# A hand-ordered S5 scan and GEGLU kernel: a filler product taken out, two transposes moved ahead of the parameters, and two loads moved back behind slab 0's first gated rows

## The chip, the cores and the metric

The kernel runs on one core of one Trainium2 chip. The metric is the device time of one execution in microseconds (us). Below, PE is the matrix engine (TensorE; PEld are its weight loads), DVE the vector engine, ACT the scalar engine, POOL GpSimd, and SP the engine that issues nearly all transfers, in the order in which the program lists them.

## What is computed

```python
x  = A_x                                  # 1 x 2048 x 512, bf16
xn = (x - mean(x)) / sqrt(var(x) + 1e-5)  # over the 512 columns
# S5 scan over the 2048 rows, state of 512 complex numbers
Lam_bar = exp(exp(log_dt) * (Lambda_re + 1j * Lambda_im))
Bu = xn @ (((Lam_bar - 1) / Lam)[:, None] * B).T
h[t] = Lam_bar * h[t - 1] + Bu[t]
s  = 2 * real(h @ C.T) + xn * Dskip
# gated feed-forward, 512 -> 1376 -> 512
g  = silu((gelu(xn @ w_gate) * (xn @ w_up)) @ w_down)
out = x + s * g
```

## The kernel before

The 2048 rows are cut into four slabs of 512 rows, and each slab into four tiles of 128 rows. Per slab the kernel normalizes the rows, turns them (columns onto partitions), multiplies them by w_up and w_gate (`gate_tile`; for slab 0 `up_rows` and `first_w`), multiplies the two results into `at`, turns `at` into `atT` by a transposing transfer (`at_t`), multiplies by w_down (`down_pair`), projects with B (`half`, which also holds the scan on DVE), and joins everything in `y_tile`.

**The order is written out by hand.** Every piece of work is a step with a number, given in the order in which `Plan.add` is called; `ORDER` lists the numbers in the order in which they are put into the program. An engine executes its own steps strictly in that order, so only the order within one engine matters; a step waits there for whatever it reads and for the buffers that it writes.

The start, where the change is. Slab 0 is not normalized before its first products: `center` subtracts the mean (tile 0 with sums on DVE and ACT, tiles 1 and 2 with a sum on ACT and the subtraction on DVE, L351), `head_t` turns the tile on PE with four small products against the identity matrix, and DVE or ACT copies the result out of PSUM into `xcT` (L322 and L324 for the two halves of tile 0, L333 for tiles 1 and 2). `up_rows(m, k)` is a pair of products of tile m with the k-th 128 rows of w_up, and can run as soon as that quarter of w_up has landed. The inverse deviation is applied when the products are copied out.

- Step 26, `dummies`: seven products of constants, before any data is there.
- Steps 30, 31: tile 0 turned on PE (L316). Step 34, `parameters` (L606, L607): log_dt and Lambda turned, into `ybank[1]`. Step 60, `fill` (L305): one product of constants into `ring[0]`, which nothing reads. Step 61: tile 1 turned (L331), into `ybank[0]`. Step 63: `up_rows(0, 0)`. Step 65: tile 2 turned, into `ybank[1]`. Step 64: `up_rows(1, 0)`; the other pairs follow.
- On DVE: step 41 (tile 1 centered, L351), 35 (the parameters copied out of `ybank[1]`, L609), 32 (first half of tile 0 copied, L322), 43 (tile 2 centered), 62 (tile 1 copied), 66 (tile 2 copied).

The loads on SP: x tiles 0 to 2, four quarters of w_up, its last columns, x tile 3, and w_gate in two parts (steps 0 to 10). Then step 115 (L686): the last 96 of w_down's 1376 rows, 96 KB; step 113 (L217): x of slab 1, 512 KB; step 116 (L687): `Drow`, the 512 values of Dskip copied to all partitions, 128 KB. Then transposing transfers: step 137 (L367), slab 0's normalized rows into `xnT`; steps 11 and 12 (L237), B's real and imaginary part into `BT`; step 152 (L468), the gated rows of tile 0 into `atT`. Step 114 (L685): w_down's first 1280 rows, 1280 KB. Steps 153 and 154: tiles 1 and 2 into `atT`. Step 224: slab 1 into `xnT`.

What uses them: PE needs `xnT` of slab 0 for `first_w(3, ...)` (L421) and for `half(0, ...)` (L550, which also needs `BT`); `down_pair(0, ...)` (L484) takes tile 0, then tile 2, then tile 1, eleven products each, the first ten with w_down's first 1280 rows and the last with the 96. `Drow` is read by `skip` on DVE (L372), steps 130, 132, 134, 136 for the four tiles of slab 0.

Of the kernel before, what the change touches and what calls it, by code (L numbers as in the profile page):

```python
# [18 lines left out]


ORDER = (
    21, 22, 23, 24, 25, 0, 27, 26, 20, 18, 19, 17, 1, 40, 15, 16, 13, 14, 2, 42, 3, 4, 5, 28, 29, 30, 31, 34, 60, 33, 44, 45, 41, 61, 35, 32, 63, 43,
    65, 62, 64, 69, 68, 66, 67, 71, 72, 46, 47, 36, 37, 38, 48, 49, 50, 52, 51, 55, 54, 129, 56, 6, 74, 77, 70, 73, 80, 75, 76, 78, 79, 53, 81, 82, 7,
    83, 85, 87, 84, 118, 86, 120, 88, 8, 57, 58, 131, 133, 59, 135, 119, 39, 194, 195, 117, 121, 122, 9, 89, 91, 93, 90, 92, 94, 10, 95, 97, 101, 103,
    107, 109, 96, 98, 102, 104, 108, 110, 115, 113, 212, 213, 216, 217, 123, 99, 100, 210, 211, 214, 215, 218, 116, 136, 132, 105, 106, 219, 130, 111,
    112, 134, 125, 124, 126, 137, 138, 140, 142, 144, 146, 148, 139, 141, 143, 145, 147, 149, 150, 151, 11, 156, 160, 175, 157, 161, 220, 225, 12,
    158, 162, 177, 179, 159, 181, 223, 163, 222, 221, 176, 178, 354, 182, 180, 164, 165, 166, 168, 167, 169, 170, 171, 172, 173, 174, 183, 152, 114,
    229, 230, 153, 154, 233, 231, 234, 224, 237, 239, 254, 271, 279, 276, 275, 272, 278, 240, 255, 232, 273, 274, 277, 280, 281, 155, 235, 241, 292,
    260, 243, 236, 242, 288, 256, 238, 196, 197, 198, 261, 298, 258, 293, 307, 289, 257, 294, 244, 299, 313, 303, 200, 184, 199, 201, 259, 296, 290,
    308, 304, 318, 295, 297, 311, 322, 309, 291, 305, 185, 187, 282, 186, 188, 226, 202, 203, 204, 314, 348, 312, 326, 328, 228, 227, 301, 300, 323,  # L30
    337, 205, 206, 207, 306, 320, 310, 324, 327, 319, 333, 286, 321, 335, 341, 283, 325, 284, 285, 329, 128, 316, 189, 208, 191, 192, 209, 193, 349,
    343, 355, 315, 190, 331, 330, 350, 360, 361, 339, 334, 127, 342, 336, 338, 356, 245, 246, 351, 362, 250, 302, 414, 422, 287, 372, 376, 374, 389,
    373, 377, 340, 378, 393, 390, 344, 391, 406, 416, 375, 379, 394, 417, 421, 415, 392, 420, 407, 345, 346, 357, 249, 248, 365, 247, 252, 253, 353,
    262, 263, 332, 410, 431, 411, 366, 432, 371, 251, 317, 352, 358, 347, 412, 439, 446, 408, 440, 419, 413, 441, 395, 418, 409, 437, 435, 447, 442,
    456, 454, 396, 436, 450, 433, 457, 438, 452, 477, 451, 471, 423, 265, 424, 425, 428, 434, 448, 467, 426, 461, 455, 475, 367, 449, 429, 453, 267,
    266, 264, 444, 476, 478, 498, 469, 269, 270, 462, 496, 268, 363, 359, 427, 443, 472, 459, 499, 468, 488, 492, 458, 368, 482, 489, 497, 493, 470,
    369, 480, 380, 381, 384, 382, 383, 463, 364, 430, 533, 473, 519, 490, 515, 474, 494, 483, 491, 520, 495, 521, 522, 516, 503, 479, 385, 464, 386,
    484, 370, 485, 500, 387, 501, 388, 397, 398, 399, 401, 402, 445, 547, 535, 517, 504, 548, 518, 509, 510, 531, 534, 532, 511, 505, 400, 404, 403,
    405, 523, 524, 527, 526, 514, 528, 465, 481, 460, 549, 486, 502, 553, 551, 537, 554, 565, 559, 552, 536, 555, 538, 550, 561, 557, 563, 560, 574,
    615, 558, 556, 570, 566, 620, 621, 572, 616, 580, 571, 564, 562, 576, 573, 587, 581, 595, 578, 585, 579, 593, 575, 589, 577, 591, 568, 594, 596,  # L40
    610, 506, 525, 512, 529, 567, 487, 583, 617, 625, 626, 608, 507, 618, 582, 622, 630, 611, 590, 592, 606, 604, 588, 586, 600, 602, 631, 609, 603,
    605, 601, 607, 530, 539, 540, 613, 597, 541, 569, 513, 623, 508, 598, 627, 466, 644, 612, 543, 544, 542, 545, 546, 632, 619, 584, 638, 636, 639,
    599, 640, 624, 633, 628, 614, 642, 645, 643, 650, 651, 637, 646, 656, 657, 641, 661, 662, 666, 667, 634, 635, 629, 647, 652, 653, 658, 659, 663,
    664, 668, 669, 648, 649, 654, 655, 660, 665, 670,
)


# [33 lines left out]
def kernel(  # L81
# [103 lines left out]
    def pe(n, cols, emit, reads=(), writes=(), **kw):  # L185
        return pl.add(PE, n * (cols + 6) / 2400.0, emit, reads, writes, lag=0.22, **kw)
# [98 lines left out]
    def rstd(m0, m1):  # L285

        def f():
            if m0 in BN:
                G.tensor_scalar(out=ve[:, m0:m1], in0=mv[:, m0, 1:2], scalar1=EPS, scalar2=None, op0=ALU.add)
            else:  # L290
                G.tensor_scalar(out=ve[:, m0:m1], in0=ss[:, m0:m1], scalar1=1.0 / D, scalar2=EPS, op0=ALU.mult, op1=ALU.add)
            G.tensor_tensor(out=rs[:, 0, m0:m1], in0=ve[:, m0:m1], in1=mhalf[:, m0:m1], op=ALU.pow)
        return pool(0.65 + 0.2 * (m1 - m0), f, [("mv", m) if m in BN else ("ss", m) for m in range(m0, m1)] + ["mhalf"], [("rs", 0, m) for m in range(m0, m1)],
             rank=250.0 - 20 * m0)
# [7 lines left out]
    def fill(k, i):  # L302
        def f():
            for _ in range(k):
                T.matmul(ring[i][:], lhsT=warm[:, 0:P], rhs=warm, start=True, stop=True)  # L305
        pe(k, 512, f, [], [("bank", i)])

    def head_t(m):

        if m == 0:  # L310
            for i in range(2):
                tp = ring[2 + i][:].bitcast(BF16)[:, 0 : D // 2].rearrange("p (k t) -> p k t", t=P)

                def f(i=i, tp=tp):
                    for k in range(2):
                        T.transpose(tp[:, k, :], xn[0][:, (2 * i + k) * P : (2 * i + k + 1) * P], ident[:])  # L316
                pe(2, P, f, [("xc", 0, i), "ident"], [("bank", 2 + i)])
            for i in range(2):
                tp = ring[2 + i][:].bitcast(BF16)[:, 0 : D // 2].rearrange("p (k t) -> p k t", t=P)
                dst = xcT[:, 2 * i : 2 * i + 2, 0:P]  # L320
                if i == 0:
                    head.append(dve(256, lambda tp=tp, dst=dst: V.tensor_copy(out=dst, in_=tp), [("bank", 2)], [("xcT", 0, 0)], rate=2.0, rank=500.0, after=head[-1:]))  # L322
                else:
                    acts(256, lambda tp=tp, dst=dst: act(out=dst, in_=tp, func=AF.Copy), [("bank", 3)], [("xcT", 0, 1)], rank=500.0)  # L324
            return
        bank, key = ybank[(m + 1) % 2], ("y", (m + 1) % 2)
        tp = bank[:].bitcast(BF16)[:, 0:D].rearrange("p (k t) -> p k t", t=P)

        def f():
            for k in range(KT):  # L330
                T.transpose(tp[:, k, :], xn[m][:, k * P : (k + 1) * P], ident[:])  # L331
        pe(KT, P, f, [("xc", m, 0), ("xc", m, 1), "ident"], [key])
        dve(512, lambda: V.tensor_copy(out=xcT[:, :, m * P : (m + 1) * P], in_=tp), [key], [("xcT", m, 0), ("xcT", m, 1)], rate=2.0, rank=310.0 - 20 * m)  # L333
# [331 lines left out]
        rstd(m, m + 1)  # L665
    stats(M - 1)
    rstd(M - 1, M)
    fill(1, 0)
    head_t(1)
    up_rows(0, 0)  # L670
    up_rows(1, 0)
# [174 lines left out]
```

## Time and profile before

| | us |
|---|---|
| median of 3 runs | 178.81 |
| the runs | 178.15 to 179.05 |
| the profiled execution, whole | 178.7 |
| its span, first to last instruction | 176.9 |

Between the span and the whole execution lie 1.8 us in which no engine of the program works. The granted clock of PE over the span has the mean 0.998. The page counts how long each engine was busy, the chain of waits follows the work back from the last instruction, and the timeline lists instructions by their start. Most packets are small ones of 256 B, those of the transposing transfers:

```profile
DMA packets 48467, 18.66 MB, mean 105 GB/s; under 512 B 40296, under 2 KB 47944, under 8 KB 48456
```

When a transfer has landed is told by the trace's completion marks, sixteen for each transfer of full width; "landed" below means the last of them.

### The profile page before, as it was taken

The numbers are of one execution on the slowest core, as the hardware profiler recorded it, in microseconds if no ns is written. First come the engines' busy times: TensorE is split into PE (matmuls) and PEld (weight loads), VectorE is DVE, ScalarE is ACT, GpSimd is POOL, SyncE is SP. The second block draws the span as 40 slices with busy tenths as digits, with TensorE's granted clock in tenths as the row PEclk, the third lists the DMA queues.
The fourth block names the chain that finished last, engine by engine and source line by source line (L and its number), as shares of the span: only waits on it lengthen the run. The fifth ranks groups of instructions, "written<-read, shape, count | busy, mean of one in ns | idle before, by whom it ended". The sixth has DMA issues, their size and how long they took to land.

```text
span 176.9 us, 2403 instructions
## 1 busy us (share of the span) xinstructions
PE 172.0 (97%) x830; PEld 82.6 (47%) x846; DVE 157.0 (89%) x252; ACT 123.8 (70%) x236; POOL 11.3 (6%) x25
## 2 busy tenths in 40 slices
PE   8999999999999999999999999999999999999992
PEld 2554554444455544444445454444444455444451
DVE  3759999999798993999979999899999999999764
ACT  6499969969999999799578855373158618582240
POOL 2660030000200000000040000000000000000000
PEclk9999999999999999999999999999999999999999
DMA  5999999997000809423000074094000007718022
GB/s 150 311 372 230 201 235 261 205 284 143 0 0 0 200 1 186 98 79 62 0 0 6 30 139 93 31 191 85 0 0 0 0 30 158 68 34 160 26 76 76
DMA packets 48467, 18.66 MB, mean 105 GB/s; under 512 B 40296, under 2 KB 47944, under 8 KB 48456
## 3 DMA queue, kind: packets, MB, share of 16 engines
q1 hardware_dynamic: 48432, 18.52, 48.7%
q8 instruction: 6, 0.10, 0.3%
q14 instruction: 5, 0.04, 0.1%
q10 hardware_dynamic: 24, 0.00, 0.0%
HBM read 6.46 MB, written 2.10 MB: 48 GB/s over the span
## 4 chain that ended last, share of the span: by engine, by line
PE 94%; DVE 2%; DMA 1%; issue 1%; DVEq 0%
PE ring L452 31%; PE ring L484 21%; PE ring L550 16%; PE ybank L500 15%; PE ring L421 5%; PE ring L391 3%; PE ybank L421 2%; DMA x_tok<-in_A_x_dram 1%; DVE yg L505 1%; DVE junk L511 1%; PE ybank L331 0%; PE ring L316 0%; DVE yg L344 0%; PE ring L305 0%; DVE xna L346 0%
## 5 line engine op out<-in xcount | busy, mean ns | idle before, releaser
L452 PEld LDWEIGHTS <-xnT 128*128 128x128 bf16 x288 | 28.2, 98 | 28.4
L484 PE MATMUL ring<-wd,atT 128*128 128x512 bf16 (+1 forms) x171 | 38.9, 379 | 0.3
L452 PE MATMUL ring<-wg,xnT 128*128 128x512 bf16 (+1 forms) x142 | 31.4, 356 | 0.1
L452 PE MATMUL ring<-wu,xnT 128*128 128x512 bf16 (+1 forms) x142 | 31.2, 356 | 0.1
L550 PE MATMUL ring<-xnT,BT 128*128 128x512 bf16 x128 | 30.1, 379 | 0.0
L581 DVE TENSOR_TENSOR_SCAN Fs<-rho,ini,W 128x512 bf16<-128x512 f32 x24 | 29.7, 1271 | 0.1
L455 ACT ACTIVATE ub<-ring 128x512 bf16<-128x512 f32 (+1 forms) x36 | 19.2, 555 | 14.1 <-PE ring L452 14.0
L500 PE MATMUL ybank<-C,hst 128*128 128x512 bf16 x115 | 27.3, 379 | 0.3
L484 PEld LDWEIGHTS <-atT 128*128 128x128 bf16 (+1 forms) x176 | 17.2, 98 | 20.8
L552 ACT ACTIVATE U<-ring 128x512 bf16<-128x512 f32 x32 | 18.2, 600 | 7.5 <-PE ring L550 7.5
L455 ACT ACTIVATE gt<-ring 128x512 bf16<-128x512 f32 (+1 forms) x36 | 19.5, 555 | 3.7 <-PE ring L452 3.5
L500 PEld LDWEIGHTS <-hst 128*128 128x128 bf16 x136 | 13.3, 98 | 14.0
L550 PEld LDWEIGHTS <-BT 128*128 128x128 bf16 x128 | 12.5, 98 | 14.7
L487 ACT ACTIVATE g<-ring 128x512 f32<-128x512 f32 x16 | 9.4, 595 | 14.2 <-PE ring L484 14.2
L562 DVE TENSOR_TENSOR Q<-U,tab 128x4096 bf16<-128x4096 bf16 x8 | 18.3, 2289 | 0.9 <-ACT tab L649 0.7
L562 DVE TENSOR_TENSOR Q<-Fs,tab 128x4096 bf16<-128x4096 bf16 x8 | 18.3, 2287 | 0.1
L505 DVE TENSOR_TENSOR yg<-ybank,g 128x512 bf16<-128x512 f32 x15 | 10.2, 686 | 5.8 <-PE ybank L500 5.7
L764 ACT ACTIVATE junk<-x_tok 128x512 bf16<-128x512 bf16 x16 | 10.0, 633 | 0.8 <-DMA x_tok<-in_A_x_dram 0.8
L496 ACT ACTIVATE ybank<-sk 128x512 f32<-128x512 bf16 x15 | 9.1, 604 | 1.7 <-DVE yg L505 1.6
L769 ACT ACTIVATE xna<-x_tok,nb,rs 128x512 bf16<-128x512 bf16 x12 | 9.5, 812 | 0.0
L581 DVE TENSOR_TENSOR_SCAN Fs<-rho,W 128x512 bf16<-128x512 f32 x8 | 9.3, 1210 | 0.1
L461 DVE TENSOR_TENSOR at<-gt,ub 128x1024 bf16<-128x1024 bf16 x12 | 8.2, 684 | 0.1
(140 smaller groups left out, 170.6 us busy)
## 6 DMA issues: line engine op xcount, KB each, us to landing
x_tok<-in_A_x_dram SPq DMA_DIRECT2D x3, 512.0 KB, 4.1
out_dram<-ot SPq DMA_DIRECT2D x11, 128.0 KB, 1.8
wd<-in_B_w_down_dram SPq DMA_DIRECT2D x1, 1280.0 KB
wu<-in_B_w_up_dram SPq DMA_DIRECT2D x4, 256.0 KB, 4.1
wg<-in_B_w_gate_dram SPq DMA_DIRECT2D x1, 864.0 KB
x_tok<-in_A_x_dram SPq DMA_DIRECT2D x4, 128.0 KB, 2.1
wg<-in_B_w_gate_dram SPq DMA_DIRECT2D x1, 512.0 KB, 6.3
out_dram<-ot SPq DMA_DIRECT2D x6, 64.0 KB, 1.6
```

What stands on the lines that cost most here:

```text
L421: T.matmul(ps[:, 0 : b - a], lhsT=lhs(k), rhs=wt[:, k, a:b], start=(k == 0), stop=(k == KT - 1))
L452: T.matmul(ps[:, 0 : b - a], lhsT=xnT[:, s % 2, m, k, :], rhs=wt[:, k, a:b], start=(k == 0), stop=(k == KT - 1))
L455: acts(b - a, lambda: act(out=dst[:, a:b], in_=ps[:, 0 : b - a], func=AF.Copy if up else AF.Gelu_apprx_tanh), [("bank", r)], [key], table= ...
L484: T.matmul(ps[:], lhsT=atT[:fs, k, m * P : (m + 1) * P], rhs=wd[:fs, k, :], start=(k == 0), stop=(k == NFT - 1))
L500: T.matmul(ps, lhsT=hst[s % 2][:, j // NPT, j % NPT, m * P : (m + 1) * P], rhs=C2[:, j // NPT, j % NPT, c0:c1], start=(j == 0 and not seed ...
L505: dve(w, lambda: V.tensor_tensor(out=yg[e][:, c0:c1], in0=ps, in1=g2[gi][:, b, c0:c1], op=ALU.mult), [key, ("g2", gi, b)], [("yg", e, c0)])
L550: T.matmul(ps[:], lhsT=BT[:, ri, k, pt * P : (pt + 1) * P], rhs=xnT[:, s % 2, :, k, :], start=(k == 0), stop=(k == KT - 1))
L552: acts(512, lambda q=q, ri=ri, ps=ps: act(out=U[ui][:, ri, q, :], in_=ps[:], func=AF.Copy), [("bank", r)], [("U", ui, q, ri)])
L562: dve(4096, lambda: V.tensor_tensor(out=Qf, in0=src.unsqueeze(1).to_broadcast(WQ), in1=table, op=ALU.mult), reads, ["Q"], rate=2.0)
L581: pl.add(DVE, 1.12 if s == 0 else 1.185, lambda ri=ri, q=q, pt=pt, first=first: V.tensor_tensor_scan(out=Fs[:, ri, q, :], data0=rho[:, pt ...
L764: acts(512, lambda i=i, fn=fn, sc=sc, m=m: act(out=junk()[:], in_=x_tok[:, s * M + m, :], func=fn, scale=sc, accum_out=sx[:, s, i, m : m + ...
L769: acts(512, lambda m=m: act(out=xn[m], in_=x_tok[:, s * M + m, :], func=AF.Identity, scale=rs[:, s, m : m + 1], bias=nb[:, s, m : m + 1]), ...
```

## The change

One step goes, and some change place; nothing else in the code differs. Steps after 60 are numbered one lower afterwards; the text keeps the numbers of before.

```diff
     stats(M - 1)
     rstd(M - 1, M)
-    fill(1, 0)
+
     head_t(1)
     up_rows(0, 0)
```

```diff
 ORDER = (
-    21, 22, 23, 24, 25, 0, 27, 26, 20, 18, 19, 17, 1, 40, 15, 16, 13, 14, 2, 42, 3, 4, 5, 28, 29, 30, 31, 34, 60, 33, 44, 45, 41, 61, 35, 32, 63, 43,
-    65, 62, 64, 69, 68, 66, 67, 71, 72, 46, 47, 36, 37, 38, 48, 49, 50, 52, 51, 55, 54, 129, 56, 6, 74, 77, 70, 73, 80, 75, 76, 78, 79, 53, 81, 82, 7,
...
+    21, 22, 23, 24, 25, 0, 27, 26, 20, 18, 19, 17, 1, 40, 15, 16, 13, 14, 2, 42, 3, 4, 5, 28, 29, 30, 31, 33, 44, 45, 41, 60, 34, 32, 62, 43, 61, 35,
+    64, 63, 68, 67, 65, 66, 70, 71, 46, 47, 36, 37, 38, 48, 49, 50, 52, 51, 55, 54, 128, 56, 6, 73, 76, 69, 72, 79, 74, 75, 77, 78, 53, 80, 81, 7, 82,
...
```

Sorted by engine, in the numbers of before (ACT and POOL keep their order):

| engine | before | after |
|---|---|---|
| PE | 30, 31, 34, 60, 61, 63, 65, 64 | 30, 31, 61, 34, 63, 65, 64 |
| DVE, start | 41, 35, 32, 43, 62, 66 | 41, 32, 43, 62, 35, 66 |
| SP | 10, 115, 113, 116, 137, 11, 12, 152, 114, 153, 154, 224 | 10, 113, 137, 11, 12, 152, 116, 114, 115, 153, 154, 224 |
| DVE, later | 214, 215, 136, 132, 105, 106, 219, 130, 111, 112, 134, 125, 124, 126, 150 | 214, 215, 105, 106, 125, 219, 111, 112, 130, 136, 134, 132, 124, 126, 150 |

Steps 214 and 215 are the statistics of slab 1, 105 and 106 the gated rows of tile 1 (L434, L436), 111 and 112 those of tile 2, 150 those of tile 3, 219 slab 1's means (L760), and 124 to 126 three passes over the rotation tables (L642).

## The prediction

> **What bounds the kernel now.** I read the page's busy times, then the chain of waits, then the start and the stretch from 12 to 34 us in the timelines of PE, DVE and SP.
>
> ```profile
> PE 172.0 (97%) x830; PEld 82.6 (47%) x846; DVE 157.0 (89%) x252; ACT 123.8 (70%) x236; POOL 11.3 (6%) x25
> PE 94%; DVE 2%; DMA 1%; issue 1%; DVEq 0%
> ```
>
> PE is the bound, and the chain has hardly a gap: from 4.03 us until the tail at 172 us PE runs on. Whatever moves PE's sequence early on moves the end by as much, unless PE then waits for something that was just in time. So two questions: how much earlier can PE be at the start, and what does it then run into?
>
> The start, as the chain and the timelines of PE and DVE show it:
>
> ```profile
> 4.03 0.61 PE ring L316 x4
> 4.71 0.61 PE L305 MATMUL ring<-const-bfloat16-1.0 128*128 128x512 bf16 x1
> 5.12 0.62 PE L331 MATMUL ybank<-ident,xna 128*128 128x128 bf16 x4
> 5.54 0.62 PE L391 MATMUL ring<-wu,W 128*128 128x512 bf16 x2
> 6.25 4.92 PE L391 MATMUL ring<-wu,W 128*128 128x512 bf16 x22
> 4.04 0.35 DVE L351 TENSOR_SCALAR xna<-x_tok,ma 128x512 bf16<-128x512 bf16 x1
> 4.82 0.17 DVE L609 CAST pf<-ybank 128x12 f32<-128x12 bf16 x1 [0.43 <-PE ybank L607]
> 4.90 0.28 DVE L322 COPY W<-ring 128x256 bf16<-128x256 bf16 x1
> 5.10 0.34 DVE L351 TENSOR_SCALAR xna<-x_tok,ma 128x512 bf16<-128x512 bf16 x1
> 5.77 0.42 DVE L333 COPY W<-ybank 128x512 bf16<-128x512 bf16 x1 [0.33 <-PE ybank L331]
> ```
>
> The reader is to see two speeds of PE. The filler (L305) holds PE from 4.71 to 5.12, 0.41 us for 512 columns; the 22 products from 6.25 come every (4.92 - 0.38) / 21 = 0.216 us, with 0.38 the last one's own length. The trace's record of the granted clock begins at 5.58 us: before it PE runs at half speed. Tile 1 is centered by 4.39 us (4.04 + 0.35), yet its transposes wait behind parameters and filler.
>
> The second stretch, on SP and PE:
>
> ```profile
> 6.52 0.91 SPq L686 DMA_DIRECT2D wd<-in_B_w_down_dram  x1
> 7.48 0.73 SPq L217 DMA_DIRECT2D x_tok<-in_A_x_dram  x1
> 8.25 1.10 SPq L687 DMA_DIRECT2D Drow<-in_A_Dskip_dram  x1
> 12.45 3.42 SPq L367 DMA_TRANSPOSE xnT<-xna  x1
> 20.88 1.74 SPq L468 DMA_TRANSPOSE atT<-at  x1
> 22.66 0.63 SPq L685 DMA_DIRECT2D wd<-in_B_w_down_dram  x1
> 23.85 7.11 SPq L468 DMA_TRANSPOSE atT<-at  x2
> 31.32 7.30 PE L484 MATMUL ring<-wd,atT 128*128 128x512 bf16 x32
> 24.00:28.50 4.50, 4.50 (x23) 2.13 (x22) 4.47 (x8) 3.27 (x7) 0.00 (x0) 1.00 0.94 268
> ```
>
> By the completion marks the transfers land in the order of issue: Drow 16.06, `xnT` 19.57, B 21.30 and 23.21, `atT` of tile 0 24.74, w_down's 1280 rows 30.18, `atT` of tile 1 32.17, of tile 2 33.18. PE's first use of `xnT` is a weight load at 19.62. L484 takes tile 2 second, eleven products after 31.32: its first product starts at 33.70, and its weights are loaded from 33.48. So `atT` of tile 2 is 0.30 us ahead of its use, `xnT` 0.05 us. Both are just in time.
>
> **The change, part by part.**
>
> *Filler out, tile 1 first (PE).* Tile 1's four transposes can start at 4.45 (centered at 4.39, and 0.055 us from DVE to PE, as between L346's end at 3.97 and the weight load at 4.02), 0.107 us each at the slow clock. The parameters' pair follows; before it came 0.25 us after the fourth transpose's start and the next product 0.14 us later, so PE is free at 5.16. The first quarter of w_up landed at 5.13 (issued 2.11, 3.0 us), so `up_rows(0, 0)` starts at about 5.18 instead of 5.54: 0.36 us. But those 0.36 us are at half speed. By 5.58 before, 0.04 us of that pair was done; after, 0.40. At the full clock that is 0.18 us, so tile 2's transposes start at 5.81 instead of 6.00. They write the bank that the parameters' copy on DVE must have left: L322 at 4.67 at the latest (after all of L316), L351 of tile 2 at 4.89 (its sum is read on ACT by 4.86), L333 at 5.16, L609 at 5.51 to 5.68: 0.1 us before it is needed. Then `up_rows(1, 0)`: before, PE waited for L333 (ended 6.195) until 6.25; now 6.04. So far 0.21 us.
>
> *What it runs into.* The fourth quarter of w_up was issued at 3.54 and landed at 8.75. Its first product is the thirteenth of the run and started at 8.85. It cannot come before about 8.77. The transfers in front of it are untouched. So **0.08 to 0.10 us** is left of the gain: take -0.10. The parameters are read later by POOL (L610 from 5.07 to about 5.75, 1.03 us long); L611 needed it only at 7.58, so 0.8 us of cover remain, and without that cover the tables come late, not PE.
>
> *96 KB and 128 KB out of the first queue.* `xnT` was issued at 12.45, when DVE had the last normalized row, and then waited behind them. At 268 GB/s (the window's last number) 229 kB are 0.86 us. `xnT`, and behind it B, land 0.9 us earlier, 1.2 at best. PE does not wait for them today, so this gives nothing but margin: cost 0, hidden behind L421 and L550. The next gated tile, step 152, waits for DVE's L436, which ended at 20.72, and SP was free at 20.78: so it is issued at 20.8 as before, now into an empty queue. Its latency was 3.86 us; the like one at 56.30 took 3.5. It lands 0.1 to 0.45 earlier.
>
> *The same 224 KB put in front of tiles 1 and 2's transposes.* Three SP instructions then stand before step 153: Drow's issue (1.10), w_down's (0.63) and the last rows' (0.91), where only w_down's stood: step 153 is ready on DVE at about 23.2, is issued at 24.3 to 25.4, and steps 154 and 224 queue behind it. The data take 0.86 us by the window, or 0.95 by w_down's own pace (1280 KB from 24.74 to 30.18, 235 KB per us). Against that 0.1 to 0.45 gained above. Drow's issue also delays w_down's by up to 1.1 us, hidden while Drow's own 0.5 us and the transposes of tile 0 occupy the queue; at worst 0.6 us of it shows. `atT` of tile 2 therefore lands between 33.18 + 0.86 - 0.45 = 33.6 and 33.18 + 0.95 + 0.6 - 0.1 = 34.6; below that only if the queue's slack at 24 us (DMA share 0.94 in the window) takes some 0.3 us, 33.3. I take 33.9, near the data term, because 22.66 to 24.74 was already covered. PE wants it at 33.48 - 0.10 = 33.38, so it stands still for 0.5 us, with 0.05 us of weight load laid bare: **+0.55**. w_down's 1280 rows land near 30.8, wanted at 31.2; the last rows are wanted only at the eleventh product, 33.3.
>
> *Skips and tables moved on DVE.* Same instructions, same sum. Skip 130 now waits for Drow (about 25.5) at 25.2; behind it are the other skips, the tables and tile 3's gated rows (29.04 before, next used by a transfer at 34.33). DVE then idles 1.17 us at 46.70 waiting for ACT, which takes up such a delay. Cost 0; without that cover, up to 0.5 us late at the scan. Slab 1's `xnT` lands near 36.3, wanted at 38.46: covered.
>
> **Sum.** 178.7 of the profiled execution (span 176.9, 1.8 around it) - 0.10 + 0.55 = 179.15, say 179.2. The profiled execution lies 0.1 below the median of the runs, within their spread of 0.9, so I leave it there.
>
> **Rivals.** (1) *No stall:* tile 2 lands by 33.4, as tile 0's transfer goes into an empty queue and Drow fills slack. For it: the 0.45; against it: 0.86 us of data for 0.3 of margin. 178.6. (2) *Slower, a serial SP:* Drow's issue is not covered, tile 2 lands at 34.6 or later and PE stands still for 1.2 us at L484: 178.7 - 0.1 + 1.25 = 179.85, up to 180.4 if the last rows' issue shows as well. For it: 1.10 is SP's slowest copy; against: that was into a full queue. It is slower than before beyond doubt once the landing passes 34.3. (3) *The clock comes later.* Between 3.7 and 5.16 us PE now has transposes only. The filler was the one full product there. If the grant moves by d, PE loses d / 2; d is at most the 4.8 us from the first product (0.76) to the grant, so up to 2.4, 1.2 in the middle: 179.8 to 181. Against it: PE is no idler than before. (4) *Faster:* `xnT` has 0.05 us of margin in this execution; in others PE may wait for it, and the change ends that. At most the runs' spread, 0.9: 177.8.
>
> On the third: the Trainium skill, "TensorE: Matmul & The Clock Gate", Part 4, says that transposes do not count as PE activity for the clock in the same way, and Part 1 puts the window at some 3.4 us; by these one more window at half speed would cost an estimated 1.7 us, 180.3. The trace has the grant 4.8 us after the first product, with the filler in between, and cannot tell.
>
> **How the numbers follow.** What a measurement of this kernel can tell is about 0.5%, 0.9 us, hence "same" is 177.9 to 179.7. Chances: the forecast 0.34 (178.8 to 179.6), no stall 0.14, serial SP 0.30, later clock 0.10, faster 0.12. Same 0.34 + 0.14 = 0.48; slower 0.30 + 0.10 = 0.40; faster 0.12. The range 178.0 to 180.4 leaves out most of the faster case and the far half of the later clock.
>
> **What would show it.** L305 gone, L331 at 4.45 and L391 at 5.18; the product of w_up's fourth quarter at 8.77; `xnT` landing before 18.8; a wait of PE in L484 near 33.4 for `atT`, about 0.5 us, and tile 2's transposes landing at 33.9. If the first L391 run starts late, or the clock's record later than 5.6, rival 3 is right; if L484 has no gap, rival 1; a forecast of a gap elsewhere I do not make, and one at L421 or L550 would prove me wrong.

## The result, and the profile after

| | before | after |
|---|---|---|
| median, us (11 runs each, side by side) | 178.73 | 179.93 |
| the runs | 178.15 to 179.18 | 179.12 to 180.39 |
| ratio after to before, 95% interval | | 1.0059 (1.0038 to 1.0080) |
| the profiled execution, whole | 178.70 | 179.34 |
| its span | 176.9 | 177.5 |

The changed kernel is slower by 0.6%, 1.2 us, and the interval is clear of 1. The profiled execution of the changed kernel took 179.34 us, 0.6 below the median, so the trace below shows 0.64 us of the loss.

The page's busy times and the shares of its chain of waits:

```profile
PE 173.4 (98%) x845; PEld 82.5 (46%) x845; DVE 156.9 (88%) x252; ACT 123.5 (70%) x236; POOL 12.7 (7%) x25
PE 78%; DVE 8%; DMA 8%; SPq 2%; POOL 1%; issue 1%; DVEq 0%
```

PE is still busy nearly throughout, but its share of the chain fell from 94% to 78%, and transfers went from 1% to 8%. The chain itself (start, length, what) says which:

```profile
22.19 4.98 DMA Drow<-in_A_Dskip_dram
27.19 1.43 DVE sk L372 x4
28.62 1.05 DVE Q L642
29.68 4.46 DMA atT<-at
34.19 4.93 PE ring L484 x22
```

PE runs on from 34.19, released by a transposing transfer into `atT`. The two DVE lines in the middle are to be read with care: the chain follows the last releaser that it can infer, and says that DVE held up the issue of that transfer. SP was issuing the transfer before it until then, as the timelines of SP and DVE show:

```profile
20.36 1.79 SPq L468 DMA_TRANSPOSE atT<-at  x1
22.19 0.58 SPq L687 DMA_DIRECT2D Drow<-in_A_Dskip_dram  x1
22.82 0.44 SPq L685 DMA_DIRECT2D wd<-in_B_w_down_dram  x1
23.30 0.66 SPq L686 DMA_DIRECT2D wd<-in_B_w_down_dram  x1
24.06 7.90 SPq L468 DMA_TRANSPOSE atT<-at  x2
```

```profile
27.19 1.43 DVE L372 TENSOR_TENSOR sk<-xna,Drow 128x512 bf16<-128x512 bf16 x4 [1.36 <-DMA Drow<-in_A_Dskip_dram]
```

Issuing is short: 0.58 us for `Drow`, 0.44 and 0.66 us for w_down's two parts. What is long is `Drow` itself, which has landed 4.98 us after its issue. Tiles 1 and 2, one piece of SP's line, took 7.90 us against 7.11 before. By the completion marks, `Drow` landed between 24.63 on the first of the sixteen marks and 27.17 on the last; w_down's 1280 rows between 28.88 and 31.25, where the marks of before all lay between 30.06 and 30.18; `atT` of tile 1 at 33.14 (32.17 before) and of tile 2 at 34.14 (33.18). `xnT` landed at 18.82 (19.57).

On PE, the start and the products with w_down:

```profile
4.45 0.61 PE L331 MATMUL ybank<-ident,xna 128*128 128x128 bf16 x4
5.13 1.03 PE L391 MATMUL ring<-wu,W 128*128 128x512 bf16 x2
6.38 4.95 PE L391 MATMUL ring<-wu,W 128*128 128x512 bf16 x22
11.16 1.36 PE L421 MATMUL ybank<-wu,W 128*128 128x352 bf16 x8
31.48 2.54 PE L484 MATMUL ring<-wd,atT 128*128 128x512 bf16 x11
34.19 4.93 PE L484 MATMUL ring<-wd,atT 128*128 128x512 bf16 x22 [0.17 <-DMA atT<-at]
```

L305 is gone. PE reaches w_up's products 0.41 us earlier (5.13 against 5.54), but the eight products that follow them, at 11.01 before, start at 11.16. Then comes the wait: the eleven products of tile 0 are done, and tile 2's first starts 0.549 us after the one before it (33.636 to 34.185) instead of some 0.22. So the 0.64 us are: PE at L484 later by 31.48 - 31.32 = 0.16, stopped there for 0.33, and 0.16 later still in two small gaps at 51.2 and 53.7, where ACT is late (its table load in L455 starts at 48.63, 47.17 before; on the way its L764 waited 1.8 us for slab 2's rows, 0.8 before, and L769 0.6 us for a skip, none before).

### The profile page after: what moved, and what is told of

Its sections match the earlier page's. It is cut to its first block, busy times and chain, and to the rows that moved or that the text cites. A ratio compares the mean times of both kernels' runs of the same rounds, so it can differ in the third digit from the quotient of the medians.

```text
span 177.5 us, 2418 instructions
## 1 busy us (share of the span) xinstructions
PE 173.4 (98%) x845; PEld 82.5 (46%) x845; DVE 156.9 (88%) x252; ACT 123.5 (70%) x236; POOL 12.7 (7%) x25
## 4 chain that ended last, share of the span: by engine, by line
PE 78%; DVE 8%; DMA 8%; SPq 2%; POOL 1%; issue 1%; DVEq 0%
PE ring L452 32%; PE ring L484 20%; PE ybank L500 15%; PE ring L550 12%; DMA x_tok<-in_A_x_dram 3%; DMA Drow<-in_A_Dskip_dram 3%; DMA atT<-at 3%; DVE Q L642 2%; DVE st L280 2%; SPq L213 1%; DVE sk L372 1%; DVE yg L505 1%; SPq L222 1%; DVE tab L642 1%; POOL rho L614 1%
## 5 line engine op out<-in xcount | busy, mean ns | idle before, releaser
L484 PE MATMUL ring<-wd,atT 128*128 128x512 bf16 (+1 forms) x176 | 39.5, 380 | 0.2 <-DMA atT<-at 0.2
L550 PE MATMUL ring<-xnT,BT 128*128 128x512 bf16 x128 | 30.1, 379 | 0.0
L455 ACT ACTIVATE ub<-ring 128x512 bf16<-128x512 f32 (+1 forms) x36 | 19.1, 555 | 13.5 <-PE ring L452 13.5
L484 PEld LDWEIGHTS <-atT 128*128 128x128 bf16 (+1 forms) x176 | 17.1, 98 | 21.3 <-DMA atT<-at 0.7
L455 ACT ACTIVATE gt<-ring 128x512 bf16<-128x512 f32 (+1 forms) x36 | 19.5, 556 | 3.7 <-PE ring L452 3.5
L550 PEld LDWEIGHTS <-BT 128*128 128x128 bf16 x128 | 12.5, 98 | 14.8
L764 ACT ACTIVATE junk<-x_tok 128x512 bf16<-128x512 bf16 x16 | 10.0, 632 | 1.8 <-DMA x_tok<-in_A_x_dram 1.8
L769 ACT ACTIVATE xna<-x_tok,nb,rs 128x512 bf16<-128x512 bf16 x12 | 9.5, 810 | 0.6 <-DVE sk L372 0.6
```

Of the source, the lines that this page charges most:

```text
L455: acts(b - a, lambda: act(out=dst[:, a:b], in_=ps[:, 0 : b - a], func=AF.Copy if up else AF.Gelu_apprx_tanh), [("bank", r)], [key], table= ...
L484: T.matmul(ps[:], lhsT=atT[:fs, k, m * P : (m + 1) * P], rhs=wd[:fs, k, :], start=(k == 0), stop=(k == NFT - 1))
L550: T.matmul(ps[:], lhsT=BT[:, ri, k, pt * P : (pt + 1) * P], rhs=xnT[:, s % 2, :, k, :], start=(k == 0), stop=(k == KT - 1))
L764: acts(512, lambda i=i, fn=fn, sc=sc, m=m: act(out=junk()[:], in_=x_tok[:, s * M + m, :], func=fn, scale=sc, accum_out=sx[:, s, i, m : m + ...
L769: acts(512, lambda m=m: act(out=xn[m], in_=x_tok[:, s * M + m, :], func=AF.Identity, scale=rs[:, s, m : m + 1], bias=nb[:, s, m : m + 1]), ...
```

## The experiments

Three theories. **T**, transfers: the loads put behind tile 0's transposing transfer bring those of tiles 1 and 2 late, and PE stops in L484. **H**, head: the loss comes from the start, through the clock or the copies moved there. **S**, skips: `Drow` holds DVE, and what is queued behind on DVE and ACT holds PE. All times are medians, each kernel beside runs of the kernel before on the same chip (178.69 in the first four, 178.63 in the last four). Where a wait is given without a fence, it is read from the times of consecutive products or from completion marks.

**The start alone.** The changed start, with the loads and skips where they were. On SP, in the numbers of before (first the changed kernel, then this one):

```diff
- 10, 113, 137, 11, 12, 152, 116, 114, 115, 153, 154, 224
+ 10, 115, 113, 116, 137, 11, 12, 152, 114, 153, 154, 224
```

> The start of the changed kernel (no filler, tile 1 turned ahead of the parameters, tile 0 copied ahead of them) with the loads and the skips of before. Theory T (transfers: the two loads put in front of tiles 1 and 2's transposes make PE stand still in L484, and nothing else costs): 178.6, between 178.3 and 178.8, with no gap of PE in L484. Rival H (head: without the filler the clock is granted later, and that is the loss): 179.5 to 179.9, the whole loss, with the clock record starting after 6.2 us.

Measured: 178.63 us (178.20 to 180.56), ratio 0.9991 (0.9955 to 1.0027). No gap in L484; tile 2's transfer landed at 33.32, and PE came to L484 at 31.36. The start neither costs the 1.2 us nor gains anything that can be told. H falls as the cause.

**The loads alone.** The other half: the start of before, with the filler, and the changed loads and skips. Against the changed kernel, without the lines of `ORDER`:

```diff
-
+    fill(1, 0)
     head_t(1)
```

> The loads and skips of the changed kernel with the start of before, filler included. Theory T: 179.7 to 180.1, the whole loss, with a gap of PE in L484 before tile 2's first product. Rival H: 178.7, no loss.

Measured: 179.81 us (179.00 to 180.45), ratio 1.0040 (1.0008 to 1.0071): the loss is here. This profiled execution took 180.45, 1.1 us more than that of the changed kernel, and has a wait that the trace above does not have. PE in its timeline, and a line of its waits (in all, times, longest):

```profile
32.19 2.54 PE L484 MATMUL ring<-wd,atT 128*128 128x512 bf16 x11 [0.35 <-DMA wd<-in_B_w_down_dram]
35.30 4.93 PE L484 MATMUL ring<-wd,atT 128*128 128x512 bf16 x22 [0.58 <-DMA atT<-at]
```

```profile
PE ring L484 <- DMA wd<-in_B_w_down_dram: 0.4, 1, 0.4
```

Two stops, not one. `Drow`, issued at 22.70, landed at 27.95; w_down's 1280 rows then landed at 32.14, so that tile 0's products started 0.73 us after the product before them, a stop of 0.52; tile 2's transfer landed at 35.26, a stop of 0.75. Together 1.26 us. Both are over when tile 2's transfer has landed, so their sum is set by that one landing.

**Tile 1 before tile 2.** If tile 2's transfer is all that PE waits for, taking tile 1 first, whose transfer lands 1 us before, should end the stop and leave the transfers and DVE as they are.

```diff
-    228, 229, 152, 153, 232, 230, 233, 223, 236, 238, 253, 270, 278, 275, 274, 271, 277, 239, 254, 231, 272, 273, 276, 279, 280, 154, 234, 240, 291,
+    228, 229, 152, 153, 230, 232, 223, 236, 238, 270, 231, 233, 253, 278, 275, 274, 271, 277, 239, 254, 272, 273, 276, 279, 280, 154, 234, 240, 291,
```

(These are the changed kernel's numbers: 230 and 232 are the products of tiles 1 and 2, 231 and 233 their copies on ACT. ACT now takes both copies ahead of slab 2's statistics, L764; in the changed kernel tile 1's came behind five passes of these.)

> The changed kernel, but PE takes tile 1 before tile 2 in L484 (steps 231 and 233 exchanged, and ACT copies tile 1 out before tile 2). Tile 1's transpose landed at 33.14 and tile 2's at 34.14 in the changed kernel, wanted at 33.4 and 35.8 in this order. Theory T: the stall shrinks to 0.1 or nothing, 178.7 to 179.0. Rival S (the skips that wait for Drow hold up DVE, and through it ACT and PE's banks, and that is the loss): no better than the changed kernel, 179.7 to 180.1.

Measured: 178.85 us (178.45 to 179.49), ratio 0.9994 (0.9965 to 1.0024). PE's timeline has no stop:

```profile
31.41 7.30 PE L484 MATMUL ring<-wd,atT 128*128 128x512 bf16 x33
```

All else stayed late: `Drow` 22.02 to 26.82, DVE waiting for it 1.2 us, tile 1's transfer landed at 33.17, tile 2's at 34.16. The two small gaps after 51 us remain, some 0.12 us. So the wait for tile 2 in L484 is the loss, and S falls, but for those 0.12 us: ACT's L769 waits 0.3 us for a skip here, its L764, which now stands behind both copies, is not among the waits, and the gaps are still there. A stop at tile 0, as the loads-alone kernel has it, would not have gone with this order; the median, 178.85, leaves no room for half a microsecond of it.

**Drow from 128 different rows.** The same 128 KB into the same tile, at the same place in the queue, but read from the first 128 rows of w_down, 1 KB each, rather than 128 times from the one 1 KB row of Dskip. The skip term is then computed from w_down's values, not from Dskip's.

The argument that differs, cut out of its line (L687):

```diff
-in_=A_Dskip.partition_broadcast(P)
+in_=B_w_down[0:P, :]
```

> The changed kernel, but Drow is filled from 128 different rows of w_down instead of 128 times the one row of Dskip: the same bytes, pieces and place in the queue; the skip term is computed from wrong values. Theory T with a slow broadcast (128 reads of one and the same 1 KB are what makes this load take 2.8 us and not the 0.5 of its size): Drow lands before 26.0, tile 2's transpose before 33.7, and the time is 178.7 to 179.2. Theory T with bytes alone (224 KB in front are the delay, wherever they are read): 179.7 to 180.1.

Measured: 178.83 us (178.37 to 180.57), ratio 1.0002 (0.9967 to 1.0037). It landed 2.66 us after its issue (22.46 to 25.12) instead of 4.98; w_down's rows landed at 30.06, tile 2's transfer at 33.26, and PE goes through:

```profile
31.44 4.92 PE L484 MATMUL ring<-wd,atT 128*128 128x512 bf16 x22
```

The loss is not the bytes. The windows (busy time and count of PE, PEld, DVE, ACT, POOL; then the clock, the DMA share, and GB/s) show it, first of the changed kernel, then of this one, then of the kernel before:

```profile
24.00:26.00 2.00, 2.00 (x12) 1.05 (x11) 1.02 (x3) 1.47 (x4) 0.78 (x1) 1.00 0.81 117
26.00:28.00 2.00, 2.00 (x11) 0.87 (x9) 0.81 (x3) 1.13 (x3) 0.00 (x0) 1.00 1.02 322
```

```profile
24.00:26.00 2.00, 2.00 (x12) 1.01 (x11) 1.35 (x5) 1.47 (x4) 0.62 (x1) 1.00 0.92 230
```

```profile
24.00:26.00 2.00, 2.00 (x12) 1.02 (x11) 2.00 (x6) 1.47 (x4) 0.00 (x0) 1.00 0.85 217
```

In the stretch in which `Drow` arrives the DMA engines are 0.81 busy and move 117 GB/s; with distinct rows 0.92 and 230. By the trace's list of packets, those of 1 KB that start in this stretch take 113 ns in the mean in the changed kernel and 65 with distinct rows. In the next stretch the changed kernel has 322 GB/s. The edit, though, changes two things, the tensor that is read and that each of its rows is read once; which of them counts is not separated, and that it is the repetition is argued.

**One load moved at a time.** Two kernels divide the 224 KB. In the first only `Drow` stands behind tile 0's transfer and the 96 rows are loaded early as before; in the second it is the other way round.

```diff
  SP of the changed kernel:  10, 113, 137, 11, 12, 152, 116, 114, 115, 153, 154
- Drow alone moved:          10, 115, 113, 137, 11, 12, 152, 116, 114, 153, 154
+ the rows alone moved:      10, 113, 116, 137, 11, 12, 152, 114, 115, 153, 154
```

> The changed kernel, but w_down's last 96 rows are loaded at their old place, ahead of slab 1; Drow alone stays behind tile 0's transpose. If the slow broadcast is the loss: 179.4 to 179.9, Drow landing at 26.8 or later, tile 2's transpose at 33.9 or later. If the loss goes by bytes (128 of the 224 KB): 179.2 or less, tile 2's transpose near 33.6.

> The changed kernel, but Drow is loaded at its old place, behind slab 1; w_down's last 96 rows alone stay behind the 1280. If the slow broadcast is the loss: 178.6 to 178.9, tile 2's transpose landing at 33.1 to 33.6. If the loss goes by bytes (96 of the 224 KB): 179.1 to 179.3.

Measured: with `Drow` alone moved 179.90 us (179.41 to 180.32; 6 runs), ratio 1.0062 (1.0041 to 1.0083); with the rows alone moved 178.80 (178.19 to 180.87), ratio 1.0018 (0.9996 to 1.0040). The whole loss comes with the one row of Dskip. In the first kernel's list of issues its time to landing, and in its windows and timeline what that does:

```profile
Drow<-in_A_Dskip_dram SPq DMA_DIRECT2D x1, 128.0 KB, 5.5
```

```profile
24.00:26.00 2.00, 2.00 (x13) 1.08 (x11) 1.02 (x3) 1.47 (x4) 0.87 (x1) 1.00 0.72 89
```

```profile
32.22 2.54 PE L484 MATMUL ring<-wd,atT 128*128 128x512 bf16 x10 [0.37 <-DMA wd<-in_B_w_down_dram]
35.18 4.93 PE L484 MATMUL ring<-wd,atT 128*128 128x512 bf16 x22 [0.43 <-DMA atT<-at]
```

89 GB/s, w_down's rows landed at 32.18, tile 2's transfer at 35.14, and the two stops of the loads-alone kernel again, 0.53 and 0.59 us. In the kernel with the rows alone moved the same window has

```profile
24.00:26.00 2.00, 2.00 (x12) 1.03 (x11) 1.07 (x5) 1.47 (x4) 0.94 (x1) 1.00 0.86 244
```

and tile 2's transfer landed at 32.76, earlier than in the kernel before, with no stop. The 96 rows cost 0.17 us by the medians, and by the interval anything from nothing to 0.7.

**The same load at its old place.** At its old place `Drow` was not slow, although there too the one row is read 128 times. In the kernel before it landed 0.39 us after slab 1, which is ahead of it in the queue (15.67, 16.06). The trace's list of packets says the same. There, 736 packets of 1 KB start between 11.4 and 16.5 us, those of w_down's 96 rows, of slab 1 and of `Drow`; none took over 88 ns, and the mean is 54. In the kernel with the rows alone moved there are 640, those of slab 1 and `Drow`; none took over 60 ns, and 617 of them started before 14.0, so at least 105 of `Drow`'s 128 fall into this quick stretch:

```profile
12.00:14.00 2.00, 1.95 (x12) 1.08 (x11) 1.10 (x13) 2.00 (x6) 1.28 (x2) 1.00 1.09 347
```

So the one row is not slow by itself: at its old place it was quick, and at the new place another tensor's rows took 2.66 us. What it is about the place was not tested: the new one is right behind a transposing transfer, the old one right behind 512 KB of x.

**The filler kept, behind the parameters.** For rival 3 of the prediction: the start-alone kernel, with one more full product among the early transposes.

```diff
 PE, in the numbers of before:
- 30, 31, 61, 34, 63, 65, 64
+ 30, 31, 61, 34, 60, 63, 65, 64
```

> The kernel head_only with the filler product put back, behind the parameters. By the prediction's working the filler's place is hidden: w_up's fourth quarter lands at 8.3 to 8.75 and holds PE to about the same point, so 178.6 to 178.8, no difference to head_only beyond 0.1. Rival H (the filler keeps the clock's grant early): 0.3 to 0.8 below head_only, with the record starting before 5.6. Rival W (the filler's place counts in full, 0.2 to 0.4): 178.9 to 179.0.

Measured: 178.78 us (178.27 to 179.47), ratio to the kernel before 1.0009 (0.9994 to 1.0025), against 178.63 without the filler (ratio 0.9991, 0.9955 to 1.0027): no difference. Its profiled execution has the record of the granted clock begin at 4.66 us. More on that below.

**Both loads right behind `xnT`.** An attempt at a place that costs nothing: `Drow` and the 96 rows behind slab 0's `xnT`, ahead of B's transfers, which PE needs from 24.4 on.

```diff
- 10, 113, 137, 11, 12, 152, 116, 114, 115, 153, 154, 224
+ 10, 113, 137, 116, 115, 11, 12, 152, 114, 153, 154, 224
```

> The changed kernel, but Drow and w_down's last rows are loaded directly behind slab 0's transpose into xnT, in front of B's two. PE does not need B before 24.4, and Drow's slow broadcast then lies in front of transposes with 2 to 3 us to spare. If the loss is only where the broadcast stands: 178.5 to 178.8, no gap of PE in L484, tile 2's transpose at 33.0 to 33.5. If any later place of the broadcast delays the whole queue as far as tile 2: 179.2 to 179.9, with a gap at L550 or L484.

Measured: 179.94 us (178.58 to 182.22), ratio 1.0059 (1.0033 to 1.0086). The first of the two outcomes expected did not come, the second did. `Drow` took 4.58 us here as well (14.85 to 19.43), again right behind a transposing transfer; in a window while it was in flight the engines were 0.57 busy and moved 78 GB/s:

```profile
16.00:18.00 2.00, 2.00 (x13) 1.08 (x11) 1.93 (x6) 1.99 (x5) 0.00 (x0) 1.00 0.57 78
```

B's parts landed at 22.30 and 24.62 (20.74 and 22.97 in the changed kernel), tile 0 at 25.88, w_down's rows at 31.70, tile 2 at 34.74. PE was in time at L550 and stopped twice in L484:

```profile
31.74 2.54 PE L484 MATMUL ring<-wd,atT 128*128 128x512 bf16 x10 [0.40 <-DMA wd<-in_B_w_down_dram]
34.79 1.47 PE L484 MATMUL ring<-wd,atT 128*128 128x512 bf16 x6 [0.51 <-DMA atT<-at]
```

What I had missed: the time lost early in the queue is still missing at its end. Tile 0's transfer lands 1.14 us later than in the kernel before, w_down's rows 1.52, tile 2's transfer 1.56, and the end is where the margin is smallest.

**Across the traces.** Where L484 has no stop, the time from its first product to the end of the execution is 178.70 - 31.32 = 147.38 before, 147.35 with the start alone, 147.36 with the rows alone moved, 147.35 with distinct rows, 147.36 with the filler kept; with tile 1 first it is 147.47, the 0.12 us of the two gaps. Whatever the others do, they do it before or in L484. None of these kernels is shown to be quicker than the one before.

## Why the prediction was right, and where not

The time forecast was 179.2 and the median is 179.93: inside the range, outside the likeliest case's own 178.8 to 179.6. The upper part of the range was there for two rivals, a serial SP and a later clock, and of these the first was not the reason and the second is not shown in the times; that the measured time lies inside is to that extent luck. The direction and the place were right, one size was not.

- **Filler out, tile 1 first: -0.10 forecast, not found.** The steps happened as worked out (L331 at 4.45; L391 at 5.13, forecast 5.18). The gain was to be capped by the fourth quarter of w_up at 8.77, and that never came to bear: the 22 products ran through from 6.38, the thirteenth near 8.97. The clock's record begins at 6.44 in this execution instead of 5.58, and at half speed 0.86 us cost 0.43, about twice the 0.18 to 0.21 that the start had gained. The products at 11.01 before (L421) start at 11.16 here; in the other six profiles without filler in its old place or a new one at 10.86 to 11.37; in the three with one at 10.66, 11.01 and 11.36. Nor is the landing of w_up's first quarter fixed, which the forecast took at 5.13: in the ten profiles it comes at 4.86 to 5.92, and two of them wait 0.5 us for it. So the start varies by more than the edit is worth.
- **Rival 3, a later clock: open in the single execution, not shown in the times.** The record begins at 4.66, 4.99 and 5.58 us with a filler, at 4.91 to 6.64 in seven profiles without. That leans to the rival, but ten executions that scatter by 2 us do not settle it, and with the start alone the time is 0.9991 (0.9955 to 1.0027) of before. The Trainium skill, "TensorE: Matmul & The Clock Gate", Part 4, which has transposes not count as activity for the clock in the same way, gave an estimate of 180.3; the start alone came to 178.63, so a whole window more at half speed is not what happens here, and the measurement decides.
- **`xnT` earlier, cost 0: right.** It landed at 18.82, 0.75 us earlier where 0.9 was forecast, and PE waited neither at L421 nor at L550. Its old margin of 0.05 us was worth nothing that the runs show, so rival 4 falls.
- **224 KB ahead of tiles 1 and 2: the mechanism right, the term too small.** "Drow's own 0.5 us" and the 0.86 to 0.95 us of data were worked out at the pace of other transfers (235 KB per us, 268 GB/s). That is the step that failed. At its new place `Drow` needed 4.58 to 5.54 us to land, and the engines moved 78 to 117 GB/s in the windows shown, where distinct rows needed 2.66 at 230. The trace of before could not tell this: there `Drow`'s packets were as quick as others. Its price is 179.93 - 178.83 = 1.1 us against distinct rows, and 179.90 - 178.63 = 1.27 with `Drow` alone moved, against the kernel before. The other 96 KB cost 0.17 by the medians, which their interval does not tell from nothing.
- **The stop in L484: +0.55 forecast at tile 2.** In the profiled execution it is 0.33 (landing 34.14, forecast 33.9), in the profiled executions of 180.45 (loads alone) and 180.32 (`Drow` alone) 0.75 and 0.59, and there a second stop of about 0.5 stands before it, at tile 0, for w_down's 1280 rows. For those I forecast a landing at 30.8 against 31.2 wanted; they came at 31.25, 32.14 and 32.18. The sum of the stops is set by tile 2's landing, 35.26 and 35.14 there against 34.14. How the changed kernel's median execution, 0.6 us longer than its profiled one, divides its loss is not known: no such execution was profiled. With tile 1 first a stop at tile 0 would remain, and that kernel's median has no room for one of 0.5.
- **Rival 2, a serial SP: near in its time (179.85), wrong in its reason.** It had `Drow`'s issue, 1.10 us, uncovered; the issue took 0.58. The engines were late, not SP.
- **Skips and tables: nearly right.** `Drow` was expected at 25.5 and came at 27.17, and DVE waited 1.36 us, against the 0.5 allowed for. The cover that I had named, DVE's idle time before its L740, did not absorb it: L740 starts at 48.16 instead of 46.70, since ACT, for which it waits, is as late. Of these 1.5 us PE felt 0.12 to 0.16. Whether ACT got them from the skips or from slab 2's rows was not taken apart; with distinct rows no skip is waited for, and the wait for slab 2's rows is 0.9 us (0.8 in the kernel before).

## What to carry to other kernels

Price a moved transfer at the place it goes to. Neither its size nor its own quick packets at the old place told what the same load costs behind a transposing transfer; moving one load at a time did. Time lost early in a busy queue can still be missing at its last, just-in-time landing: ask of that landing first. And one profiled execution need not show the whole loss: here tile 2's transfer landed at 34.14 in the changed kernel's, and at 34.74 to 35.26 in those of three related kernels.

## What the hardware showed that I had not expected

- Reading one 1 KB row 128 times into 128 partitions, right behind a transposing transfer, took 4.58 to 5.54 us from issue to landing in five executions; 128 different rows of another tensor took 2.66 us in one. Behind a load of 512 KB, packets of the same row took at most 88 ns in the kernel before, against 113 in the mean of the 1 KB packets at 24 to 26 us in the changed one.
- How far the sixteen marks of a transfer spread goes with what comes behind it. w_down's lie within 0.12 us where a transposing transfer is next, in the kernel before (30.06 to 30.18) and also right behind the slow load (32.08 to 32.18, `Drow` alone moved). Where the 96 rows are next they spread over 2.4 us behind the slow load (28.88 to 31.25), 1.3 behind distinct rows and 1.15 with `Drow` at its old place.
- The start of the clock's record differs by 2 us between executions of nearly the same start (4.66 to 6.64 us), which at half speed is up to 1 us of PE's time.
